# Dense layers that take a batch's tokens in the order in which the last Fourier stage makes them

## The chip, the cores and the metric

The kernel runs on one core of one Trainium2 chip. The metric is the device time of one execution in microseconds; lower is better. Engines are named as the profile names them: PE (TensorE; PEld are its weight loads), DVE (VectorE), ACT (ScalarE), POOL (GpSimd) and SP (SyncE, which here only issues DMAs).

## The reference, cut to what matters

```python
def _attn_ref(x, filt_r, filt_i):                # x: (8, 3008, 256)
    X = np.fft.rfft(x, axis=1)
    Y = X * (filt_r + 1j * filt_i)[None, :, :]
    return np.fft.irfft(Y, n=x.shape[1], axis=1)

def _moe_ref(x, w_in, w_out):                    # x: (24064, 256); 256 -> 2048 -> 256
    h = x @ w_in
    g = 0.5 * h * (1.0 + erf(h / np.sqrt(2.0)))
    return g @ w_out
```

Each of the 8 batches is filtered along its 3008 positions in the frequency domain, and then every position ("token") goes through two dense layers with an exact Gelu between them. The dense layers treat each token by itself, so they may take the tokens in any order, if each result is stored in its own row.

## The kernel before, in words

**Fourier part.** 3008 is 47 x 64. The transform and its inverse are made of small matrix products. Batch 0 has its own code (`c1` to `c4`), which runs before the main loop. Batches 1 to 7 are computed in four stages that lie between the dense layers' matmuls:

- `s1(b, c)`, four chunks: eight matmuls into four PSUM banks (three of pool `f`, one of pool `h`), drained to `a_sb` by DVE and ACT, and stored by SP to a DRAM buffer `R1`. `r1` loads it back in another layout (`b_sb`).
- `s2(b, p)`, twelve units: two matmuls into one `f` bank; DVE multiplies it with the filter `F` (line 428) into `p`.
- `s3(b, u)`, three units: sixteen matmuls into three `f` banks and one `h` bank; `s3_out` drains them to `v_sb` in two halves, the second half one slot later, and SP stores them to a DRAM buffer `R2`. `r2(b, c)` loads it back as `d_sb`, in four chunks.
- `s4(b, grp, half)`, sixteen units (8 groups of 4 columns, times 2 halves of the channels): four matmuls of 94 columns into one `f` bank, drained by DVE or ACT into the ring `y_sb`.

A token's place in its batch is 32 m + w, with m from 0 to 93 and w from 0 to 31. One `s4` group makes the four values of w from 4 grp to 4 grp + 3 for all 94 m. In the kernel before, the drain puts them at their natural places: runs of four elements, 32 apart. So a dense tile of 512 tokens in a row needs all eight groups.

**Dense part.** The tokens of all batches are cut into 47 tiles of 512 (`TCH`); 5.875 tiles make a batch, so most batches begin within a tile. `mm1(t, jc)` makes one sixteenth of tile t's hidden layer: two matmuls of 512 columns from the ring into an `h` bank and a Gelu on ACT into `g_sb` (line 589). The second layer is done by `mm2_seven` with seven block products in the place of eight: 112 matmuls of 128 columns a tile on PE (line 659) and sums of quarters on DVE (`sums_1` to `sums_3`, lines 628, 634, 641). The results are gathered by DVE in `t_sb` and `ost` (lines 674 to 688) and stored by SP, two stores of 256 rows for each tile (line 690).

**Order.** The order of every engine's work is written out by hand. The main loop has 16 slots for each tile. In slot 16 t + jc the kernel first issues what `put` has noted for that slot, then seven matmuls of `mm2_seven(t - 1)`, then `mm1(t, jc)`. Tile 5, the first to hold tokens of batch 1, is an exception: its `mm1` begins only at slot 86, and in the slots 80 to 85 the second layer of tile 4 goes twice as fast. `first(b)` is the first slot of the first tile that holds tokens of batch b. All of `s4(b)` ends before that slot:

```python
            s1, n1, r1, s2, n2, group, r2, s4, n4 = hi - 94, 3.7, hi - 80, hi - 71, 3.4, 14, hi - 25, hi - 17, 1
        unit = lambda p: s2 + group * (p // 4) + int(n2 * (p % 4))
        for u in range(16):
            put(s4 + int(u * n4), m.s4, b, u // 2, u % 2)
```

Each engine works in the order in which the instructions were issued to it. SP's one queue holds, in this order of issue, the `R1` and `R2` stores, the `r1` and `r2` loads and the stores of the result. PSUM has 3 banks for `h`, 2 for `ps_o`, 3 for `f`; the `f` banks are shared by `s1` to `s4`.

Of the kernel before, what the change touches and what calls it, by code (L numbers as in the profile page):

```python
# [20 lines left out]
HB = 32  # L21
RND = 12582912.0
TCH = 512
TURNS = 64.0


def _dram(src, off, dims):
    return dataclasses.replace(src, offset=src.offset + off, ap=[list(d) for d in dims])


class _Mix:
# [433 lines left out]
    def s4(self, b, grp, half):  # L465
        nc = self.nc
        o = b % 2 * self.S
        d = self.st[b, "d", grp // 2]
        ps = self.bank("ps_s4")
        for i in range(4):  # L470
            nc.tensor.matmul(ps[:, 94 * i:94 * i + 94],  # L471
                             lhsT=d[:, (grp % 2) * 4 + i, 128 * half:128 * half + 128],
                             rhs=self.T4a[:, 4 * grp + i], start=True, stop=True)
        yv = self.ring[:, half, o:o + self.S].rearrange("c (m w) -> c m w", w=HB)[:, :, 4 * grp:4 * grp + 4]
        pv = ps[:, 0:376].rearrange("c (i m) -> c m i", i=4)
        self._evac(yv, pv, "act" if half or b == 1 and grp > 3 else False, 1.0 / self.S)

# [75 lines left out]
    def c4(self, u, eng):  # L553

        if u == 0:

            self.ring = self.py.tile([128, 2, 2 * self.S], BF16, tag="y", name="y_sb")
        d = self.st[0, "d", u // 2]
        for half in range(2):
            ps = self.bank("ps_c4", "h" if (2 * u + half) % 5 < 3 else "o")  # L560
            for i in range(4):
                self.nc.tensor.matmul(ps[:, 94 * i:94 * i + 94],
                                      lhsT=d[:, 4 * (u % 2) + i, 128 * half:128 * half + 128],
                                      rhs=self.T4c.rearrange("p a b -> p (a b)"), start=True, stop=True)
            yv = self.ring[:, half, 0:self.S].rearrange("c (m w) -> c m w", w=HB)[:, :, 4 * u:4 * u + 4]
            self._evac(yv, ps[:, 0:376].rearrange("c (i m) -> c m i", i=4), eng[half], 1.0 / self.S)


# [22 lines left out]
    def mm2(self, t, s):  # L591
        nc = self.nc
        tile_i, q = s // 4, s % 4
        g = self.st["g", t]
        if s % 8 == 0:
            self.st["o"] = self.bank("ps_o", "o").rearrange("p (a b) -> p a b", a=2)
        ps = self.st["o"]
        for i in range(4):
            jc = 4 * q + i
            nc.tensor.matmul(ps[:, tile_i % 2, :], lhsT=g[:, jc, tile_i * 128:tile_i * 128 + 128],  # L600
                             rhs=self.w_out_sb[:, jc, :], start=(jc == 0), stop=(jc == 15))
        if s % 8 == 7:
            ost = self.po.tile([128, 2, 256], FP32, tag="ost", name="ost")
            nc.vector.tensor_copy(out=ost, in_=ps)
            r0 = t * TCH + (tile_i - 1) * 128
            nc.sync.dma_start(out=self.out[r0:r0 + 256, :].rearrange("(s p) o -> p s o", p=128), in_=ost)

    def weight_sums(self):

# [33 lines left out]
    def mm2_seven(self, t, lo, hi):  # L643

        nc, v = self.nc, self.nc.vector.tensor_tensor
        a11, a12, s2, a22 = self.quarters(t)
        w = self.w_out_sb.rearrange("p (i k) (n o) -> p k n i o", k=2, n=2)
        q = self.w_sums
        s31, s4 = self.st["s", t], self.st.get(("s4", t))
        ops = ((a11, w[:, 0, 0]), (a12, w[:, 1, 0]), (s2, q[:, 1]), (s31[:, :, 0], q[:, 2]),  # L650
               (s31[:, :, 1], q[:, 0]), (a22, q[:, 3]), (s4, w[:, 1, 1]))
        last = t == self.B * self.S // TCH - 1
        for n in range(lo, hi):
            m, sub, i = n // 16, n // 8 % 2, n % 8
            if n % 16 == 0 and (m == 0 or m % 2 == 1) or last and m > 4 and i == 0:
                self.st["o"] = self.bank("ps_o", "h" if n > 80 else "o").rearrange("p (m s o) -> p m s o", m=2, s=2)
            ps = self.st["o"]
            a, b = ops[m]
            nc.tensor.matmul(ps[:, (m + 1) % 2, sub, :], lhsT=a[:, i, 128 * sub:128 * sub + 128], rhs=b[:, i],  # L659
                             start=i == 0, stop=i == 7)  # L660
            if last and m > 4 and i == 7:
                self.finish(t, m, sub, ps)
            if n % 16 != 15 or m % 2 or last and m > 4:
                continue
            p0, p1 = ps[:, 0], ps[:, 1]
            if m == 0:
                self.st["t"] = self.po.tile([128, 2, 2, 128], FP32, tag="ost", name="t_sb")
                self.st["c"] = [None, None]
            if m in (2, 4):
                self.st["c"][m // 4] = self.po.tile([128, 2, 256], FP32, tag="ost", name="ost")  # L670
            t1, t3 = self.st["t"][:, 0], self.st["t"][:, 1]
            c = lambda h, k: self.st["c"][h][:, :, 128 * k:128 * k + 128]
            if m == 0:
                nc.vector.tensor_copy(out=t1, in_=p1)
            elif m == 2:
                v(out=c(0, 0), in0=t1, in1=p0, op=ALU.add)  # L676
                if last:
                    self.store(t, 0, 0, nc.sync)
                v(out=t1, in0=t1, in1=p1, op=ALU.add)
            elif m == 4:  # L680
                v(out=t3, in0=t1, in1=p0, op=ALU.subtract)  # L681
                v(out=c(1, 1), in0=t3, in1=p1, op=ALU.add)
                if last:
                    self.store(t, 1, 1, nc.scalar)
                v(out=t1, in0=t1, in1=p1, op=ALU.add)
            else:
                for h, tt, p in ((1, t3, p0), (0, t1, p1)):
                    v(out=c(h, 1 - h), in0=tt, in1=p, op=ALU.add)  # L688
                    r0 = t * TCH + 256 * h
                    nc.sync.dma_start(out=self.out[r0:r0 + 256, :].rearrange("(s p) o -> p s o", p=128),  # L690
                                      in_=self.st["c"][h])

    def store(self, t, h, k, eng):
        r0, k = t * TCH + 256 * h, slice(128 * k, 128 * k + 128)
        eng.dma_start(out=self.out[r0:r0 + 256, k].rearrange("(s p) o -> p s o", p=128), in_=self.st["c"][h][:, :, k])

    def finish(self, t, m, sub, ps):

        h = 6 - m
        c, tt = self.st["c"][h], self.st["t"][:, h]  # L700
        k = slice(128 * (1 - h), 128 * (1 - h) + 128)
        self.nc.vector.tensor_tensor(out=c[:, sub, k], in0=tt[:, sub], in1=ps[:, (m + 1) % 2, sub], op=ALU.add)
        if h == 1:
            if sub == 1:
                self.store(t, 1, 0, self.nc.sync)
            return
        r0 = t * TCH + 128 * sub
        (self.nc.sync if sub else self.nc.scalar).dma_start(out=self.out[r0:r0 + 128, k], in_=c[:, sub, k])


@with_exitstack
def kernel(
# [9 lines left out]
    m = _Mix(ctx, tc, x, filt_r, filt_i, moe_w_in, moe_w_out, out)  # L722
    nc, B, S = tc.nc, m.B, m.S
# [114 lines left out]
    def put(slot, f, *a):  # L838
        at.setdefault(slot, []).append((f, a))
# [4 lines left out]
    for b in range(1, B):  # L844
        hi = first(b)
        if b == 1:
            s1, n1, r1, s2, n2, group, r2, s4, n4 = 0, 3, 12, 27, 2.5, 12, 64, 73, 0.75
        elif b == 2:
            s1, n1, r1, s2, n2, group, r2, s4, n4 = hi - 92, 3.7, hi - 78, hi - 70, 3.4, 14, hi - 24, hi - 17, 1
        else:  # L850
            s1, n1, r1, s2, n2, group, r2, s4, n4 = hi - 94, 3.7, hi - 80, hi - 71, 3.4, 14, hi - 25, hi - 17, 1
        unit = lambda p: s2 + group * (p // 4) + int(n2 * (p % 4))
        for u in range(16):
            put(s4 + int(u * n4), m.s4, b, u // 2, u % 2)
        for c in range(4):
            put(s1 + int(c * n1), m.s1, b, c)
            put(r1 if c < 3 else unit(3) + 1, m.r1, b, c)
            put(r2 if c < 3 else s4 + int(4 * n4) + 1, m.r2, b, c)
        for p in range(12):
            put(unit(p), m.s2, b, p)  # L860
            if p % 4 == 3:
                put(unit(p) + 3, m.s3, b, p // 4)
                put(unit(p) + 4, m.s3_out, b, p // 4, 1)
        if b + 1 < B:
            for i in range(8):
                put(unit(i + 2) if b > 1 else 25, m.load_next, b, i + 2, i // 2, i % 2)
# [20 lines left out]
    for s in range((NT + 1) * 16):  # L887
        t, jc = s // 16, s % 16
# [41 lines left out]
```

## Time and profile before

| | |
|---|---|
| median of 3 runs | 751.09 us (751.04 to 751.09) |
| the profiled execution: its time | 751.4 us |
| the profiled execution: its span, first to last instruction | 749.5 us |
| mean granted clock of TensorE | 0.999 |
| busy share of PE, DVE, ACT, POOL | 97%, 79%, 73%, 14% |
| Gelu, `g_sb<-ps_h`, 752 of 512 columns | 599 ns each |
| drain of `s4`, `y_sb<-ps_s`, 376 columns | 545 ns on DVE, 481 ns on ACT |
| filter product `p<-ps_s,F` on DVE (84) | 1220 ns each |
| stores of the result on SP | 92 of 256 KB, 3.0 us to landing, and three smaller at the end |
| `d_sb<-R` on SP (56) | 192 KB, 3.9 us to landing |
| DMA issues on SP, all | 333 |

The span is some 2 us less than the execution's time, since launch and end lie around it. The profile's busy time of PE is made from modelled ends of matmuls, so the distance from one start to the next says more than a duration. A line number is that of the kernel before; helper lines stand for many callers (303, 305 and 307 are the drains of `_evac`), so tiles are named with them.

### The profile page before, as it was taken

The numbers are of one execution on the slowest core, as the hardware profiler recorded it, in microseconds if no ns is written. First come the engines' busy times: TensorE is split into PE (matmuls) and PEld (weight loads), VectorE is DVE, ScalarE is ACT, GpSimd is POOL, SyncE is SP. The second block draws the span as 40 slices with busy tenths as digits, with TensorE's granted clock in tenths as the row PEclk, the third lists the DMA queues.
The fourth block names the chain that finished last, engine by engine and source line by source line (L and its number), as shares of the span: only waits on it lengthen the run. The fifth ranks groups of instructions, "written<-read, shape, count | busy, mean of one in ns | idle before, by whom it ended". The sixth has DMA issues, their size and how long they took to land.

```text
span 749.5 us, 20005 instructions
## 1 busy us (share of the span) xinstructions
PE 729.1 (97%) x8286; PEld 517.9 (69%) x8420; DVE 588.9 (79%) x1053; ACT 548.6 (73%) x975; POOL 105.2 (14%) x195
## 2 busy tenths in 40 slices
PE   7999999999999999999999999999999999999998
PEld 4855666766776667666777666666677766777776
DVE  7978866897787977789777996779967798666566
ACT  6986678777786778766787667876678767777773
POOL 7979100020001200012000120002100000000000
PEclk9999999999999999999999999999999999999999
DMA  9998653565354652546625557245562432501011
GB/s 150 219 221 241 151 142 93 165 127 118 92 129 142 142 130 80 157 118 120 148 71 157 112 106 170 61 146 121 125 142 72 135 107 76 124 29 58 30 57 58
DMA packets 90187, 90.70 MB, mean 121 GB/s; under 512 B 6768, under 2 KB 76912, under 8 KB 89840
## 3 DMA queue, kind: packets, MB, share of 16 engines
q1 hardware_dynamic: 82000, 72.18, 34.9%
q0 software_dynamic: 7680, 17.04, 14.5%
q8 instruction: 66, 1.08, 0.6%
q10 hardware_dynamic: 416, 0.20, 0.1%
q14 instruction: 25, 0.20, 0.1%
HBM read 57.15 MB, written 48.23 MB: 141 GB/s over the span
## 4 chain that ended last, share of the span: by engine, by line
PE 84%; DVE 6%; DMA 4%; ACT 2%; issue 2%; POOL 0%; SPq 0%; DVEq 0%; POOLq 0%; ACTq 0%
PE ps_o L659 36%; PE ps_h L586 35%; PE ps_s L471 3%; PE ps_s L442 3%; PE ps_s L425 2%; PE ps_s L398 2%; DVE p L428 2%; DVE s_sb L628 2%; DMA R<-v_sb 2%; ACT g_sb L589 2%; DMA d_sb<-R 2%; DMA x_sb<-in_x_dram 1%; PE ps_c L533 1%; PE ps_c3t L548 1%; PE ps_c L511 0%
## 5 line engine op out<-in xcount | busy, mean ns | idle before, releaser
L589 ACT ACTIVATE g_sb<-ps_h 128x512 f16<-128x512 f32 x752 | 446.6, 599 | 181.9 <-PE ps_h L586 158.7
L586 PE MATMUL ps_h<-y_sb,w_in_sb 128*128 128x512 bf16 (+3 forms) x1470 | 417.5, 365 | 0.4
L659 PEld LDWEIGHTS <-g_sb 128*128 128x128 f16 x2944 | 193.9, 98 | 78.8 <-issue 14.8
L659 PEld LDWEIGHTS <-s_sb 128*128 128x128 f16 x2208 | 150.0, 98 | 51.6 <-issue 3.5
L586 PEld LDWEIGHTS <-w_in_sb 128*128 128x128 bf16 x1600 | 124.8, 98 | 8.0 <-issue 1.0
L659 PE MATMUL ps_o<-w_sums,g_sb 128*128 128x128 f16 x1472 | 127.3, 219 | 1.2 <-DVE g_sb L634 0.4
L659 PE MATMUL ps_o<-w_sums,s_sb 128*128 128x128 f16 x1472 | 125.8, 219 | 1.2
L628 DVE TENSOR_TENSOR s_sb<-g_sb 128x1024 f16<-128x1024 f16 x184 | 123.5, 695 | 0.3 <-ACT g_sb L589 0.3
L659 PE MATMUL ps_o<-w_out_sb,g_sb 128*128 128x128 f16 x1472 | 119.8, 219 | 2.1 <-DVE ost L688 0.4
L428 DVE TENSOR_TENSOR p<-ps_s,F 128x1024 bf16<-128x1024 f32 x84 | 102.5, 1220 | 20.3 <-PE ps_s L425 19.0
L122 POOL COPY gate<-p 1x1 bf16<-1x1 bf16 x40 | 18.7, 468 | 416.5 <-DVE p L428 416.5
L634 DVE TENSOR_TENSOR g_sb<-s_sb,g_sb 128x1024 f16<-128x1024 f16 x92 | 63.6, 691 | 1.1
L659 PE MATMUL ps_o<-w_out_sb,s_sb 128*128 128x128 f16 x736 | 63.8, 219 | 0.5
L641 DVE TENSOR_TENSOR s_sb<-g_sb 128x1024 f16<-128x1024 f16 x92 | 63.0, 684 | 0.0
L307 DVE TENSOR_SCALAR y_sb<-ps_s 128x376 bf16<-128x376 f32 x52 | 28.3, 545 | 27.7 <-PE ps_s L471 27.7
L471 PEld LDWEIGHTS <-d_sb 96*128 96x128 bf16 x448 | 31.2, 98 | 26.4 <-issue 2.6
L681 DVE TENSOR_TENSOR t_sb<-t_sb,ps_o 128x256 f32<-128x256 f32 x46 | 19.2, 416 | 38.3 <-PE ps_o L659 38.3
L305 DVE CAST a_sb<-ps_s 128x512 bf16<-128x512 f32 x57 | 36.6, 686 | 14.8 <-PE ps_s L398 14.6
L676 DVE TENSOR_TENSOR ost<-t_sb,ps_o 128x256 f32<-128x256 f32 x46 | 19.3, 419 | 33.6 <-PE ps_o L659 33.4
L471 PE MATMUL ps_s<-T4a,d_sb 96*128 96x94 bf16 x448 | 37.4, 206 | 2.7 <-DMA d_sb<-R 1.4
L688 DVE TENSOR_TENSOR ost<-t_sb,ps_o 128x256 f32<-128x256 f32 x90 | 33.6, 414 | 6.4 <-PE ps_o L659 6.4
L86 POOL DMA_DIRECT2D x_sb<-in_x_dram x64 | 32.9, 520 | 3.1 <-issue 2.9
(148 smaller groups left out, 508.7 us busy)
## 6 DMA issues: line engine op xcount, KB each, us to landing
out_dram<-ost SPq DMA_DIRECT2D x92, 256.0 KB, 3.0
x_sb<-in_x_dram POOLq DMA_DIRECT2D x64, 188.0 KB, 3.8
b_sb<-R SPq DMA_DIRECT2D x28, 384.0 KB, 4.0
R<-v_sb SPq DMA_DIRECT2D x84, 128.0 KB, 2.5
d_sb<-R SPq DMA_DIRECT2D x56, 192.0 KB, 3.9
R<-a_sb SPq DMA_DIRECT2D x54, 192.0 KB, 3.0
F<-Fd SPq DMA_DIRECT2D x4, 512.0 KB, 9.7
Fd<-F SPq DMA_DIRECT2D x8, 192.0 KB, 6.9
```

The costliest lines, as they stand in the source:

```text
L86: nc.gpsimd.dma_start(out=xt[h * o:h * o + NA, w:w + 8, :], in_=xv[h][:, w:w + 8, :])
L305: self.nc.vector.tensor_copy(out=out, in_=in_)
L307: self.nc.vector.tensor_scalar(out=out, in0=in_, scalar1=scale, scalar2=None, op0=ALU.mult)
L428: nc.vector.tensor_tensor(out=w, in0=ps.unsqueeze(1).to_broadcast([128, 2, 512]), in1=self.F[:, :, 2 * p:2 * p + 2, :].rearrange("p t a b ...
L471: nc.tensor.matmul(ps[:, 94 * i:94 * i + 94], lhsT=d[:, (grp % 2) * 4 + i, 128 * half:128 * half + 128], rhs=self.T4a[:, 4 * grp + i], sta ...
L586: nc.tensor.matmul(ps[:, o:o + n], lhsT=w[:, dc], rhs=self.ring[:, dc, off:off + n], start=(dc == 0), stop=(dc == 1))
L589: nc.scalar.activation(out=self.st["g", t][:, jc, :], in_=ps, func=AF.Gelu)
L628: self.nc.vector.tensor_tensor(out=self.st["s", t][:, i:i + 2], in0=a, in1=b, op=ALU.subtract)
L634: self.nc.vector.tensor_tensor(out=a21[:, k], in0=self.st["s", t][:, k, 0], in1=a22[:, k], op=ALU.add)
L641: self.nc.vector.tensor_tensor(out=self.st["s4", t][:, k], in0=a12[:, k], in1=s2[:, k], op=ALU.subtract)
L659: nc.tensor.matmul(ps[:, (m + 1) % 2, sub, :], lhsT=a[:, i, 128 * sub:128 * sub + 128], rhs=b[:, i], start=i == 0, stop=i == 7)
L688: v(out=c(h, 1 - h), in0=tt, in1=p, op=ALU.add)
```

## The change

- Within the ring a batch's tokens now stand group by group: group `grp` is the 376 places from `GRP * grp` (94 m times 4 w). The `s4` and `c4` drains write 376 elements in a row.
- A dense tile of 512 places needs the one, two or three groups that it touches. `s4` is spread over the tiles: `due(u)` is the first slot of the first tile that uses group u, and its two halves are put 3 slots apart, the first of them 5 to 14 slots ahead of it (1 for batch 1's first). `r2` of chunk c comes 9 slots (8 for the last chunk) before the first group that uses it. So `s4` of a batch now lies in the same slots as `s1`, `s2` and `s3` of the next one.
- `s1`, `s2`, `s3` and their loads start 6 slots later for batches 2 to 7; for batch 1 the `s2` units stand 3 slots apart in groups of 14 slots, in the place of 2.5 and 12.
- The results of a tile belong to rows of the output in groups of four. `put_rows` stores 128 places at a time, cut where a group ends: runs of four rows of 1 KB, 32 rows apart. There are 253 stores of results in the place of 95; 249 are issued by SP and 4, at the end, by ACT (2 before).

The diff, without the three other places where `put_rows` takes the place of a store (`mm2`, `store`, `finish`):

```diff
+GRP = 376
...
@@ s4
-        yv = self.ring[:, half, o:o + self.S].rearrange("c (m w) -> c m w", w=HB)[:, :, 4 * grp:4 * grp + 4]
+        o += GRP * grp
+        yv = self.ring[:, half, o:o + GRP].rearrange("c (m w) -> c m w", w=4)
@@ c4
-            yv = self.ring[:, half, 0:self.S].rearrange("c (m w) -> c m w", w=HB)[:, :, 4 * u:4 * u + 4]
+            yv = self.ring[:, half, GRP * u:GRP * u + GRP].rearrange("c (m w) -> c m w", w=4)
@@ mm2_seven
-                    r0 = t * TCH + 256 * h
-                    nc.sync.dma_start(out=self.out[r0:r0 + 256, :].rearrange("(s p) o -> p s o", p=128),
-                                      in_=self.st["c"][h])
+                    for sub in range(2):
+                        self.put_rows(t * TCH + 256 * h + 128 * sub, self.st["c"][h][:, sub], nc.sync)
+
+    def put_rows(self, r0, tile_, *engines, k=slice(0, 256)):
+
+        lo, hi = r0, r0 + 128
+        for eng in engines * 4:
+            if lo == hi:
+                return
+            b, i = divmod(lo, self.S)
+            n = min(hi - lo, GRP - i % GRP)
+            o = b * self.S + 4 * (i // GRP) + HB * (i % GRP // 4)
+            w = k.stop - k.start
+            out = _dram(self.out, o * self.D + k.start, [[HB * self.D, n // 4], [self.D, 4], [1, w]])
+            eng.dma_start(out=out, in_=tile_[lo - r0:lo - r0 + n])
+            lo += n
+        assert lo == hi
@@ the kernel's schedule
         if b == 1:
-            s1, n1, r1, s2, n2, group, r2, s4, n4 = 0, 3, 12, 27, 2.5, 12, 64, 73, 0.75
+            s1, n1, r1, s2, n2, group = 0, 3, 12, 27, 3, 14
         elif b == 2:
-            s1, n1, r1, s2, n2, group, r2, s4, n4 = hi - 92, 3.7, hi - 78, hi - 70, 3.4, 14, hi - 24, hi - 17, 1
+            s1, n1, r1, s2, n2, group = hi - 86, 3.7, hi - 72, hi - 64, 3.4, 14
         else:
-            s1, n1, r1, s2, n2, group, r2, s4, n4 = hi - 94, 3.7, hi - 80, hi - 71, 3.4, 14, hi - 25, hi - 17, 1
+            s1, n1, r1, s2, n2, group = hi - 88, 3.7, hi - 74, hi - 65, 3.4, 14
         unit = lambda p: s2 + group * (p // 4) + int(n2 * (p % 4))
-        for u in range(16):
-            put(s4 + int(u * n4), m.s4, b, u // 2, u % 2)
+
+        due = lambda u: (b * S + GRP * u) // TCH * 16
+        pair = lambda u: 0 <= u < 7 and due(u + 1) == due(u)
+        s4 = lambda u: due(u) - ((1 if b == 1 else 10 if pair(0) else 5) if u == 0 else 14 if pair(u) else
+                                 5 if pair(u - 1) else 8)
+        for u in range(8):
+            for half in range(2):
+                put(s4(u) + 3 * half, m.s4, b, u, half)
         for c in range(4):
             put(s1 + int(c * n1), m.s1, b, c)
             put(r1 if c < 3 else unit(3) + 1, m.r1, b, c)
-            put(r2 if c < 3 else s4 + int(4 * n4) + 1, m.r2, b, c)
+            put(s4(2 * c) - (9 if c < 3 else 8), m.r2, b, c)
```

More of the change, by code (lines that the diff above doesn't have):

```diff
@@ L604, in mm2 @@
             nc.vector.tensor_copy(out=ost, in_=ps)
-            r0 = t * TCH + (tile_i - 1) * 128
-            nc.sync.dma_start(out=self.out[r0:r0 + 256, :].rearrange("(s p) o -> p s o", p=128), in_=ost)
+            for sub in range(2):
+                self.put_rows(t * TCH + (tile_i - 1 + sub) * 128, ost[:, sub], nc.sync)
     def weight_sums(self):
@@ L688, in mm2_seven @@
                     v(out=c(h, 1 - h), in0=tt, in1=p, op=ALU.add)
-                    r0 = t * TCH + 256 * h
-                    nc.sync.dma_start(out=self.out[r0:r0 + 256, :].rearrange("(s p) o -> p s o", p=128),
-                                      in_=self.st["c"][h])
+                    for sub in range(2):
+                        self.put_rows(t * TCH + 256 * h + 128 * sub, self.st["c"][h][:, sub], nc.sync)
[12 more added lines that the diff above has]
+        assert lo == hi
     def store(self, t, h, k, eng):
-        r0, k = t * TCH + 256 * h, slice(128 * k, 128 * k + 128)
-        eng.dma_start(out=self.out[r0:r0 + 256, k].rearrange("(s p) o -> p s o", p=128), in_=self.st["c"][h][:, :, k])
+        k = slice(128 * k, 128 * k + 128)
+        for sub in range(2):
+            self.put_rows(t * TCH + 256 * h + 128 * sub, self.st["c"][h][:, sub, k], eng, k=k)
     def finish(self, t, m, sub, ps):
@@ L706, in finish @@
             return
-        r0 = t * TCH + 128 * sub
-        (self.nc.sync if sub else self.nc.scalar).dma_start(out=self.out[r0:r0 + 128, k], in_=c[:, sub, k])
+        engines = (self.nc.sync, self.nc.scalar)
+        self.put_rows(t * TCH + 128 * sub, c[:, sub, k], *(engines if sub else engines[::-1]), k=k)
 @with_exitstack
```

## The prediction

> **What bounds the kernel now.** First the page: its totals and the chain that ended last.
>
> ```profile
> span 749.5 us, 20005 instructions
> PE 729.1 (97%) x8286; PEld 517.9 (69%) x8420; DVE 588.9 (79%) x1053; ACT 548.6 (73%) x975; POOL 105.2 (14%) x195
> ...
> PE 84%; DVE 6%; DMA 4%; ACT 2%; issue 2%; POOL 0%; SPq 0%; DVEq 0%; POOLq 0%; ACTq 0%
> ```
>
> TensorE is the bound: 97% busy, 84% of the chain. Second the stretches, to see where TensorE does more than its pure work: two batches from first Gelu to first Gelu, one tile without Fourier work, and two tiles of a batch's middle (columns: stretch, its length, busy us of PE, PEld, DVE, ACT, POOL, clock, DMA share, GB/s).
>
> ```profile
> 206.94:297.64 90.70, 89.79 (x1050) 64.68 (x1064) 73.93 (x131) 66.99 (x119) 7.56 (x16) 1.00 0.50 123
> ...
> 388.25:479.72 91.47, 89.78 (x1050) 65.54 (x1064) 73.93 (x131) 66.97 (x119) 7.56 (x16) 1.00 0.51 122
> 674.91:688.07 13.16, 13.05 (x146) 9.38 (x146) 8.00 (x18) 9.55 (x16) 0.00 (x0) 1.00 0.12 41
> ...
> 236.69:252.06 15.37, 15.14 (x167) 10.44 (x168) 14.67 (x26) 10.60 (x18) 4.36 (x10) 1.00 0.68 148
> 267.41:282.02 14.61, 14.45 (x170) 10.04 (x171) 10.49 (x23) 10.91 (x20) 0.00 (x0) 1.00 0.64 154
> ```
>
> Six pure tiles are 6 x 13.16 = 79.0 us, so a batch's transform adds 11.7 us to 90.7. Of that `s4` is 64 matmuls that start 47 ns apart, 3.0 us: full rate, no wait. A batch from 2 on has nothing to gain by spreading `s4`. VectorE is 95% busy in the stretch 236.69 to 252.06 (`s2`, `s3`) and 72% in the next but one, where `s4` starts. Third the timeline: where TensorE really waits.
>
> ```profile
> 69.85 0.62 PE L442 MATMUL ps_s<-p,U 64*64 64x512 bf16 x7 [0.83 <-DVE p L428]
> ...
> 71.02 0.51 PE L659 MATMUL ps_o<-w_sums,g_sb 128*128 128x128 f16 x6 [0.38 <-DVE g_sb L634]
> ...
> 83.66 0.62 PE L442 MATMUL ps_s<-p,U 64*64 64x512 bf16 x7 [1.02 <-ACT v_sb L303]
> ...
> 106.51 0.51 PE L471 MATMUL ps_s<-T4a,d_sb 96*128 96x94 bf16 x8 [0.41 <-DMA d_sb<-R]
> ...
> 118.32 1.05 PE L398 MATMUL ps_s<-x_sb,T1s 47*64 47x512 bf16 x8
> 118.43 0.49 ACT L303 ACTIVATE y_sb<-ps_s 128x376 bf16<-128x376 f32 x1 [0.48 <-PE ps_s L471]
> ...
> 207.66 0.63 PE L398 MATMUL ps_s<-x_sb,T1s 47*64 47x512 bf16 x8
> ...
> 461.86 0.34 PE L471 MATMUL ps_s<-T4a,d_sb 96*128 96x94 bf16 x4 [0.83 <-DMA d_sb<-R]
> ```
>
> By start-to-start gaps against the normal step, these are 1.1, 0.6, 1.3, 0.4 (batch 1) and 0.8 us (batch 5). The rows at 118.32, 118.43 and 207.66 are the price that I use most: eight `s1` matmuls take 0.63 us, but 1.05 us where an `s4` unit stands just before them, since they wait until ScalarE has emptied its bank: **0.42 us**. Everything to be won is some 6 us.
>
> **What the Trainium skill says.** "PSUM — Partial Sum Buffer", Specifications: eight banks, a matmul's output fits one. The kernel uses 3 + 2 + 3; the 1.05 us row agrees that three `f` banks are few. "Perfetto Trace Analysis", Tensor Engine Instruction: the end of a matmul is estimated, and ScalarE and VectorE are strict FIFO; hence I count starts, and a drain waits for what is queued before it (at 207.77 a Gelu begins 0.1 us after `s1`, and its drains only after it). "DMA: Bandwidth & Descriptors", Latency and other measured facts: the receipt round trip to the memory dominates a DMA's fixed cost. It agrees: 128 KB of `v_sb` land after 2.5 us, 256 KB of output after 3.0. So more, smaller stores cost issue time, not latency.
>
> **The change, part by part.** Slots are the steps of the main loop (0.82 us pure); what is put at a slot runs before that slot's own matmuls.
>
> *At nothing:* the contiguous ring write. ScalarE takes 481 ns for 376 elements and 599 for 512, 0.87 ns an element; VectorE 545 and 686, 1.04: no sign of a charge for the 8-byte runs. No gain, no loss; 0.05 us each way would hide behind TensorE. Bytes and 1 KB rows of the stores stay. Matmul counts stay.
>
> *Gains, batch 1.* `s2` starts come at 27, 30, 33, 36 instead of 27, 29, 32, 34, groups of 14 slots instead of 12. VectorE, continuously busy from 59.2 to 71 (the row at 69.85 ends that), gets 1.65 us but has to do one `g_sb` (1.24) and a copy (0.41) before the last product: the wait for `p` stays 1.1, the 0.6 for `g_sb` goes. The 1.3 at 83.66 is an `s3` whose third `f` bank is its own first one; in the changed program's bank assignment it gets three different ones: -1.3. The `s1` row at 118.32: -0.4. Waits for `d_sb`: `r2` of chunk 0 alone instead of three together, and in batches 3 to 5 18 slots from the last `s3_out` to `s4` instead of 12: -0.2, -0.8, -0.1. A wait of 0.35 for L688 in the last batch: gone. Sum **-3.7** (0 to -6).
>
> *Losses: `s4` among `s1`, `s2`, `s3` of the next batch, on three `f` banks.*
> (a) An `s4` in the slot of an `s1`, whose third `f` bank is the one `s4` just filled: slots 184, 187, 280, 283, 379, 475, 568, 571. Five are VectorE drains, 0.42 + 0.06 = 0.48; three are ScalarE drains behind a running Gelu, 0.6: **+4.2** (2 to 6).
> (b) Slots 427 and 523: `s4`, then `s2` on the very same bank. VectorE starts 0.24 after the last matmul (118.19 to 118.43) and drains for 0.55: +0.8 each, **+1.6** (1 to 3).
> (c) Slots 126, 235, 331, 619: `s2` after `s4` after `s3` takes the bank that VectorE drains second (0.69 each), where before it had one drained by ScalarE: 0.4 at 126, where an L628 lies between, 0.15 elsewhere: **+0.85** (0 to 3).
> (d) Slots 139, 440, 536, 632: `s4` before `s3`, needed nine matmuls (0.6 us) later: **+0.9** (0 to 2).
> (e) VectorE: `y_sb` drains (0.55 each, one or two a tile) now fall into the 95% busy tiles; slots gain only 0.2 of TensorE each: **+0.7** (0 to 5).
> (f) Slots 80 to 82, where `mm2` runs at double rate: three `s4` units (0.19 each) no longer stand ahead of the `g_sb` that VectorE ended at 116.69, TensorE used at 116.75: **+0.55** (0 to 1).
>
> *Stores.* 95 become 253 (249 on SP, 4 on ScalarE's queue at the end); SP issues 487 DMAs instead of 333. Back to back they take 0.48 us each (449.28, 449.77), so five or six stores hold SP for 2.5 to 3 us, not 1. Behind them queue `R` writes and `r2`. `r2` at the slot after the stores (144, 608, 704; chunk 3): stores begin 0.56 us after the Gelu of that slot, five of them and two loads end 3.6 us in, landing 3.9 later (the median): 7.5 us, when `s4` is due eight slots (6.7 us and what else is in them) later: 0.35, 0.15, 0.75: **+1.2** (0 to 3). Two slots later they have 2 us to spare. The wait of a store for VectorE holds only SP. The tail stays: the last two stores go on two queues.
>
> Sum: 4.2 + 1.6 + 0.85 + 0.9 + 0.7 + 0.55 + 1.2 = 10.0; less 3.7, **+6.3 us**. The profiled execution is 751.4 us (span 749.5), the median 751.09; 751.1 + 6.3 = **757.4 us**.
>
> **The rivals.** *Faster:* the drains come back in time, so that (a) to (d) cost a third, 2.5 us, (e) and stores nothing, and batch 1 loses even its 1.1: 751.1 - 4.8 + 3.0 = 749.3, at best 746. For it: before, no wait from batch 2 on is long. It decides where a drain ends within the 0.4 us of five `s1` matmuls; the row at 118.32 speaks against. *VectorE becomes the bound:* each of six batches loses 1 us more in the `s2` tiles, since 14.67 + 0.55 of 15.37 us leaves nothing: 763. *SP becomes the bound:* ten `r2` are issued within two slots after five or six stores; at 0.6 us an issue and the longest landing of `d_sb` (5.6 us) each would be 1 to 2 us late: 770. Against it: q1 holds the 16 engines for 34.9% of the span only, and seven of the ten have 2 us of slack. *Nothing to measure:* losses at their lower ends equal the gains, 751.
>
> **How the numbers follow.** A measurement tells about 0.2%, 1.5 us, from no change. Likeliest case (752.6 to 761) 0.49, VectorE 0.14, SP 0.10: slower 0.73. Within 1.5 us 0.10. Faster 0.17. The likeliest case's own range is 753 to 761; the range for 8 in 10 leaves out half of the faster case and most of SP's: 748.5 to 764.
>
> **What would show it.** Right: in the waits, `ps_s` L399 waiting for `y_sb` drains, `ps_s` L426 too; batches 2 to 5 near 92 us instead of 90.7; the tile with `s4`'s old place shorter (15.6 to about 14), the `s2` tiles longer; the 83.66 row gone; L705 with 249 issues on SP. Wrong: batch periods of 90.7 or less mean that the drains are hidden; waits for `d_sb` over 1 us mean SP; p L429 and ost L690 among what TensorE waits for mean VectorE.

## The result, and the profile after

The changed kernel takes **767.59 us** (median; 767.15 to 768.39) beside 751.07 us (750.62 to 751.09) of the kernel before: ratio 1.0223 [1.0205, 1.0240], 16.5 us slower. The forecast was slower by 6.3 us, at most 764: right in sign, wrong in size.

The page of the kernel after: its totals and the chain that ended last.

```profile
span 765.8 us, 20240 instructions
PE 736.9 (96%) x8286; PEld 520.2 (68%) x8420; DVE 586.3 (77%) x1053; ACT 550.1 (72%) x975; POOL 103.2 (13%) x195
...
PE 74%; DVE 10%; DMA 7%; issue 3%; ACT 2%; POOL 2%; SPq 1%; DVEq 0%; POOLq 0%; ACTq 0%
```

TensorE does the same matmuls (8286 recorded in both profiles) in a span 16.3 us longer; its share of the chain falls from 84% to 74%, VectorE's rises from 6% to 10% and that of DMAs from 4% to 7%. Some 3 points of TensorE's fall and 2 of the DMAs' rise lie ahead of the main loop, where the chain only takes another path: the first Gelu stands at 39.31 us, before at 39.41. The rest is waiting. The list of waits of the kernel after names it (columns: total us, times, longest; PEld and PE on the same line are mostly the same wait seen twice):

```profile
PEld L661 <- DVE g_sb L636: 6.8, 13, 1.7
PEld L472 <- DMA d_sb<-R: 6.6, 4, 1.9
...
PE ps_s L472 <- DMA d_sb<-R: 4.9, 5, 1.4
...
PE ps_s L426 <- DVE y_sb L308: 1.3, 2, 0.6
...
PE ps_s L399 <- ACT y_sb L304: 1.0, 3, 0.3
```

The rows of the kernel before that belong to the first two:

```profile
PE ps_s L471 <- DMA d_sb<-R: 1.4, 3, 0.8
...
PEld L659 <- DVE g_sb L634: 0.8, 2, 0.5
```

The waits of `s1` (L399) and `s2` (L426) for `y_sb` drains are the bank waits that the prediction was about. The list shows only a part of them, since it counts idle time behind the modelled ends of matmuls; from start to start they are 5.6 us. The waits of `s4` (L472) for `d_sb` were to be over 1 us only if SP was the trouble: it was. Next the stretches (columns as in the prediction's table): of the kernel after two batches, a tile with two `s4` units and nothing else, and the last tile; then the last tile of the kernel before:

```profile
207.07:299.82 92.75, 91.05 (x1050) 64.85 (x1064) 73.50 (x131) 67.43 (x119) 6.89 (x16) 1.00 0.50 120
392.53:485.08 92.55, 90.61 (x1050) 65.97 (x1064) 73.70 (x131) 67.25 (x118) 7.16 (x16) 1.00 0.50 120
686.28:699.80 13.52, 13.36 (x153) 9.75 (x154) 8.55 (x19) 9.93 (x17) 0.00 (x0) 1.00 0.25 69
742.45:765.83 23.38, 18.23 (x238) 14.56 (x238) 13.47 (x30) 9.45 (x16) 0.00 (x0) 0.98 0.23 69
```

```profile
727.55:749.50 21.95, 18.52 (x243) 14.79 (x243) 13.76 (x31) 9.56 (x16) 0.00 (x0) 0.98 0.23 74
```

The first of the two batches takes 92.75 us instead of 90.70, the second 92.55 instead of 91.47 (forecast: near 92). The tile with two `s4` units takes 13.52, one without any took 13.16: 0.18 each, their bare work. Up to tile 11 nothing is lost (its first Gelu stands at 207.07, before at 206.94): what batch 1 gains pays for what is lost up to there. The end loses 1.43 us that no term of the sum had. Two kinds of stall in the timeline of the kernel after; first an `s4` just ahead of an `s1` (left: start, duration):

```profile
216.47 0.34 PE L472 MATMUL ps_s<-T4a,d_sb 96*128 96x94 bf16 x4
...
216.74 0.62 PE L399 MATMUL ps_s<-x_sb,T1s 47*64 47x512 bf16 x5
217.17 0.48 ACT L304 ACTIVATE y_sb<-ps_s 128x376 bf16<-128x376 f32 x1
...
217.69 0.41 PE L399 MATMUL ps_s<-x_sb,T1s 47*64 47x512 bf16 x3 [0.34 <-ACT y_sb L304]
```

`s1` stops after five matmuls until the drain that stood behind a Gelu is done; start to start the sixth comes 0.65 us late. Then `r2` behind the stores:

```profile
712.37 0.76 DVE L690 TENSOR_TENSOR ost<-t_sb,ps_o 128x256 f32<-128x256 f32 x2 [0.39 <-PE ps_o L661]
...
712.82 3.92 SPq L705 DMA_DIRECT2D out_dram<-ost  x5
...
716.84 1.10 SPq L463 DMA_DIRECT2D d_sb<-R  x2
...
720.62 0.35 PE L472 MATMUL ps_s<-T4a,d_sb 96*128 96x94 bf16 x4 [1.27 <-DMA d_sb<-R]
```

Five stores hold SP for 3.92 us, the two loads follow, and TensorE goes on 3.8 us after the first of them was issued; in the kernel before such a load landed after 3.9 (median), so it isn't the load that is slow here. The prediction had the same five stores at 0.48 us each, 2.4 in all.

### The profile page after: what moved, and what is told of

The parts are those of the page before. It is cut to its first block, busy times and chain, and to the rows that moved or that the text cites. A ratio compares the mean times of both kernels' runs of the same rounds, so it can differ in the third digit from the quotient of the medians.

```text
span 765.8 us, 20240 instructions
## 1 busy us (share of the span) xinstructions
PE 736.9 (96%) x8286; PEld 520.2 (68%) x8420; DVE 586.3 (77%) x1053; ACT 550.1 (72%) x975; POOL 103.2 (13%) x195
## 3 DMA queue, kind: packets, MB, share of 16 engines
q8 instruction: 66, 1.08, 0.6%
## 4 chain that ended last, share of the span: by engine, by line
PE 74%; DVE 10%; DMA 7%; issue 3%; ACT 2%; POOL 2%; SPq 1%; DVEq 0%; POOLq 0%; ACTq 0%
PE ps_o L661 33%; PE ps_h L588 32%; DVE s_sb L630 3%; DMA d_sb<-R 3%; PE ps_s L472 3%; PE ps_s L443 3%; DVE p L429 2%; PE ps_s L399 2%; DVE g_sb L636 2%; ACT g_sb L591 2%; DMA x_sb<-in_x_dram 2%; PE ps_s L426 1%; POOL x_sb L87 1%; DMA F<-in_filt_i_dram 1%; DMA R<-v_sb 1%
## 5 line engine op out<-in xcount | busy, mean ns | idle before, releaser
L661 PEld LDWEIGHTS <-g_sb 128*128 128x128 f16 x2944 | 196.9, 98 | 84.8 <-DVE g_sb L636 6.8
L661 PEld LDWEIGHTS <-s_sb 128*128 128x128 f16 x2208 | 147.4, 98 | 53.2 <-issue 10.3
L661 PE MATMUL ps_o<-w_sums,g_sb 128*128 128x128 f16 x1472 | 128.9, 219 | 5.5 <-DVE g_sb L636 3.0
L123 POOL COPY gate<-p 1x1 bf16<-1x1 bf16 x40 | 16.7, 418 | 432.7 <-DVE p L429 432.7
L472 PEld LDWEIGHTS <-d_sb 96*128 96x128 bf16 x448 | 31.3, 98 | 30.7 <-DMA d_sb<-R 6.6
L472 PE MATMUL ps_s<-T4a,d_sb 96*128 96x94 bf16 x448 | 37.9, 206 | 5.9 <-DMA d_sb<-R 4.9
L690 DVE TENSOR_TENSOR ost<-t_sb,ps_o 128x256 f32<-128x256 f32 x90 | 33.7, 417 | 8.0 <-PE ps_o L661 8.0
L426 PE MATMUL ps_s<-b_sb,T2p 128*128 128x256 bf16 x168 | 32.0, 272 | 1.9 <-DVE y_sb L308 1.3
```

The lines of the kernel that those rows point to most:

```text
L426: nc.tensor.matmul(ps[:, 256 * i:256 * i + 256], lhsT=self.T2p[:, k].rearrange("p a b c d -> p (a b c d)"), rhs=self.st[b, "b", k // 6][:, ...
L472: nc.tensor.matmul(ps[:, 94 * i:94 * i + 94], lhsT=d[:, (grp % 2) * 4 + i, 128 * half:128 * half + 128], rhs=self.T4a[:, 4 * grp + i], sta ...
```

## The experiments

All times are medians with the ratio to the kernel before, which took 750.7 to 751.07 us beside them.

**r2_early**: the loads away from the stores, nothing else.

```diff
-            put(s4(2 * c) - (9 if c < 3 else 8), m.r2, b, c)
+            put(s4(2 * c) - (13 if c else 9), m.r2, b, c)
```

> Kernel after, but the loads r2 of chunks 1 to 3 of every batch are issued 13 slots ahead of their s4 instead of 9 or 8, so that none stands on SP behind the five or six stores of a tile half or behind a wait for R1. Theory SP (the loads of d_sb are late because the stores occupy SP's queue just ahead of them): the four long d_sb waits (184.14, 611.18, 633.68, 720.62 us; 1.34 + 1.09 + 0.85 + 1.22 us beyond the normal step) go, so 767.6 - 4.5 = 763 us (762 to 764.5). Rival, traffic (the loads land late because the transfers themselves are slow, whatever SP's order): the waits stay, 766.5 to 768.

Measured: 762.87 us, 1.0157 [1.0141, 1.0172]; 4.7 us less than the kernel after. The four long waits are gone. By the starts of the Gelus around them they were 1.55, 1.30, 1.08 and 1.45 us, 5.4 in all and some 0.2 more each than the expectation has; two other waits came out 0.4 longer each, one of them in batch 1, whose first load was not moved (109.70 us). Loads issued four or five slots sooner would have hidden slow transfers too, so this run alone doesn't tell SP's order from them; the next one, where the loads keep their slots and their bytes, does for the waits that it takes away.

**stores_before**: the stores of the kernel before, the schedule of the kernel after.

```diff
-            for sub in range(2):
-                self.put_rows(t * TCH + 256 * h + 128 * sub, self.st["c"][h][:, sub], nc.sync)
+            r0 = t * TCH + 256 * h
+            nc.sync.dma_start(out=self.out[r0:r0 + 256, :].rearrange("(s p) o -> p s o", p=128), in_=self.st["c"][h])
...
```

> Kernel after with the stores of the kernel before: one DMA of 256 consecutive rows for each half tile (the results so land in rows in another order than the reference's). SP issues 158 fewer DMAs. Theory SP: the d_sb waits that stand behind stores shrink (some 3 of 4.5 us; the one at 611 us stands behind a wait for R1 and stays), and the end, where the last store lands 4.5 us after VectorE's last sum instead of 2.8, comes 1.4 to 1.7 us nearer: 762.5 to 763.5 us. Rival, the stores cost nothing of their own (order of s4 is all): 767 to 768.

Measured: 762.11 us, 1.0147 [1.0132, 1.0163]. The last tile is back at 21.94 us, and of the waits for `d_sb` those at the slots 152 and 594 are left in part (0.95 and 1.03 us); those at 616 and 712 are gone. At 152 the first load is issued at 178.06 and TensorE goes on only 5.9 us later, so there the loads themselves have a part. So in this schedule the new stores cost 5.5 us, and the schedule with the old stores costs 11.0. The wait at 594 is mostly not the stores' doing: there `r2` stands behind three loads `b_sb` of 384 KB, and TensorE gets its data only 6.3 us after the first `d_sb` load is issued (604.87 to 611.18 in the kernel after).

**dodge**: `s4` out of the slots of `s1`, `s2`, `s3`.

```diff
-                put(s4(u) + 3 * half, m.s4, b, u, half)
+                late_s4.append((s4(u) + 3 * half, b, u, half))
...
+    busy = {s for s in at for f, a in at[s] if f in (m.s1, m.s2, m.s3)}
+    for s, *a in late_s4:
+        put(s + (s in busy), m.s4, *a)
```

> Kernel after, but an s4 unit whose slot holds an s1, s2 or s3 too is put one slot later (same work, same engines). Theory banks (terms a to d of the prediction: TensorE waits for the f bank that s4 has just filled): s1 waits 4.2, s2 waits 1.6 + 0.6 and s3 waits some 1 us go for the most part: 767.6 - 6 = 761.5 us (760.5 to 764). Rival, VectorE is the limit in these tiles: what the banks give back is lost in waits for g_sb: 766 to 768.

Measured: 761.12 us, 1.0144 [1.0127, 1.0162]; 6.5 us less, on four runs from 759.80 to 763.11. The timeline of dodge at the place shown above: `s1` runs clear, and the `s4` has the time after it.

```profile
212.51 0.63 PE L399 MATMUL ps_s<-x_sb,T1s 47*64 47x512 bf16 x8
...
213.91 0.34 PE L472 MATMUL ps_s<-T4a,d_sb 96*128 96x94 bf16 x4
```

The gain isn't lost to VectorE.

**order_only**: the new token order and the new stores, every other stage where the kernel before has it.

```diff
-            s1, n1, r1, s2, n2, group = hi - 88, 3.7, hi - 74, hi - 65, 3.4, 14
+            s1, n1, r1, s2, n2, group, r2, s4, n4 = hi - 94, 3.7, hi - 80, hi - 71, 3.4, 14, hi - 25, hi - 17, 1
...
+        for u in range(16):
+            put(s4 + int(u * n4), m.s4, b, u // 2, u % 2)
```

> The schedule of the kernel before (s1, s2, r2, s4 in their old slots, s4 in one run) with the new token order and the new stores of groups of four rows. Theory (s4 spread is most of the loss, the stores cost only where r2 stands behind them and at the end): 751.1 + 1.4 (end) + 0 to 1.5 = 752.5 to 754 us. Rival, the stores alone are the loss (SP's queue late everywhere): 758 or more. Rival, the stores cost nothing: 751.

Measured: 770.02 us, 1.0258 [1.0242, 1.0273]. My number missed by 16 us, and the rival that I had put at 758 or more holds. The waits that order_only adds are of one sort:

```profile
PE ps_s L472 <- DMA d_sb<-R: 10.9, 6, 3.6
...
PEld L472 <- DMA d_sb<-R: 5.1, 3, 1.9
...
PE ps_s L426 <- DMA b_sb<-R: 4.8, 4, 1.9
```

Both loads that come over SP, `r1` and `r2`, are late in nearly every batch; tile 11, where `s1` stands clear of `s4`, takes 15.83 us (before: 15.88). With stores and schedule both old or new there are four kernels:

| | old stores | new stores |
|---|---|---|
| old schedule | 751.1 | 770.0 |
| new schedule | 762.1 | 767.6 |

The new stores cost 19.0 us on the old schedule and 5.5 on the new one. The new schedule (`s4` and `r2` spread, `s1` to `s3` moved) costs 11.0 by itself and hides 13.5 of what the stores cost.

**before_253**: why a store is dear. The kernel before, its stores cut into the same pieces but with consecutive rows.

```diff
+            n = min(hi - lo, GRP - lo % self.S % GRP)
+            eng.dma_start(out=self.out[lo:lo + n, k], in_=tile_[lo - r0:lo - r0 + n])
```

> Kernel before, its stores cut into the same 253 pieces as the kernel after has, but of consecutive rows (output as the reference's). In the kernel after an issue of a store takes SP 0.71 us on the mean (249 make 176.9 us), in the kernel before 0.45 (90 make 40.9 us). Theory form (the four-row pattern makes an issue longer): here a store takes about 0.45 again, 112 us of SP, and the time lies well below order_only's 770: 753 to 760 us. Rival, number (an issue close behind another is slow, whatever its rows): about 0.7 us a store and the same late loads as in order_only: 768 to 771.

Measured: 755.55 us, 1.0058 [1.0043, 1.0073]. The means below are of SP's 249 store records in each trace:

| SP, one store | pieces of 128 rows (128) | shorter pieces (121) | all |
|---|---|---|---|
| consecutive rows (before_253) | 0.46 us | 0.45 us | 0.455 us, sum 113.4 us |
| groups of four rows (after) | 0.62 us | 0.80 us | 0.711 us, sum 176.9 us |

Five stores in a row, in the timeline of before_253, to be read beside the five of 3.92 us above:

```profile
452.20 2.10 SPq L700 DMA_DIRECT2D out_dram<-ost  x5
```

The number of issues costs 4.8 us on the old schedule, their form the other 14.5 up to order_only.

**after_flat**: the same edit of the row pattern in the kernel after.

```diff
-            out = _dram(self.out, o * self.D + k.start, [[HB * self.D, n // 4], [self.D, 4], [1, w]])
-            eng.dma_start(out=out, in_=tile_[lo - r0:lo - r0 + n])
+            eng.dma_start(out=self.out[lo:lo + n, k], in_=tile_[lo - r0:lo - r0 + n])
```

> Kernel after, each of its 253 store pieces written to consecutive rows instead of groups of four (the results so land in another order than the reference's). Theory form (the number of issues was priced rightly and the price of one wrongly): a store takes SP 0.45 us as in before_253, so the waits for d_sb at the slots 152, 616 and 712 shrink to about what the prediction summed (1.2 us), and the end comes nearer: 763 us (762 to 764.5). Rival (the number alone makes r2 late): 766 to 768.

Measured: 763.16 us, 1.0162 [1.0148, 1.0176]; 4.4 of the stores' 5.5 us are the form. With a store at about the price that the prediction used, the waits at the slots 152, 616 and 712 are 0.68, 0 and 1.30 us beyond the normal step (the median step between the same two kinds of matmul), together 2.0 (predicted: 1.2); at 594 there is 0.83 left. The one at 712 isn't a matter of price: one of the five stores ahead of it took 2.05 us, and the trace doesn't show why.

**combo**: dodge and r2_early together (both edits above).

> Kernel after with both edits, s4 off the slots of s1, s2 and s3 (dodge, -6.5 us) and r2 of chunks 1 to 3 earlier (r2_early, -4.7 us). Theory (two separate causes): they add up, 767.6 - 11.2 = 756.4 us (755.5 to 758). Rival (one hides behind the other, or VectorE takes over): 759 to 761.

Measured: 755.83 us, 1.0069 [1.0057, 1.0081]; 11.8 us less than the kernel after, beside 4.7 + 6.5 = 11.2. The causes are separate. The longest row of what is left among TensorE's waits, here of combo and then of the next experiment:

```profile
PEld L661 <- DVE g_sb L636: 7.2, 14, 1.7
```

```profile
PEld L661 <- DVE g_sb L636: 4.7, 10, 1.4
```

**combo_act**: combo, and VectorE drains no `y_sb` in the main loop.

```diff
-            self._evac(yv, pv, "act" if half or b == 1 and grp > 3 else False, 1.0 / self.S)
+            self._evac(yv, pv, "act", 1.0 / self.S)
```

> combo, with all y_sb drains on ScalarE instead of half on VectorE. Theory (term e: the eight waits of 0.3 to 0.4 us and one of 0.5 for g_sb from batch 2 on come from y_sb drains in VectorE's queue): these go, -2.5 us, 753.3 us (752.5 to 754.5). Rival (ScalarE's drains then hold the Gelus and TensorE waits for ps_h or for the bank instead): 756 or more.

Measured: 753.01 us, 1.0028 [1.0018, 1.0037]; 2.8 us less than combo. From batch 2 on four waits for `g_sb` are gone (1.4 us); one of 0.3 us is left in each of the batches 3 to 6, one of 0.5 in batch 2 and one of 0.1 in batch 7, and TensorE waits for no `ps_h`. The rest of the gain is other waits, those of batch 1 and of two `s1` among them. One that is left, in the timeline of combo_act:

```profile
236.45 1.22 DVE L429 TENSOR_TENSOR p<-ps_s,F 128x1024 bf16<-128x1024 f32 x1
...
237.58 0.68 DVE L636 TENSOR_TENSOR g_sb<-s_sb,g_sb 128x1024 f16<-128x1024 f16 x1
...
238.31 0.34 PEld L661 LDWEIGHTS <-g_sb 128*128 128x128 f16 x6 [0.36 <-DVE g_sb L636]
```

Here the sum stands behind a filter product of `s2`, not behind a drain. This is the best version with the new order, and still slower than the kernel before.

**combo_tail** and **combo_end**: the end. In combo_tail POOL issues the stores of tile 45, in combo_end also the first two of tile 46.

```diff
-                                      nc.sync)
+                                      nc.gpsimd if t == self.B * self.S // TCH - 2 else nc.sync)
...
-                    self.store(t, 0, 0, nc.sync)
+                    self.store(t, 0, 0, nc.gpsimd)
...
-                    self.store(t, 1, 1, nc.scalar)
+                    self.store(t, 1, 1, nc.gpsimd)
```

> combo, and the stores of the last tile but one are issued by POOL, so that SP has only the last tile's behind it at the end. Theory (the end is late because eleven stores hold SP for 8.2 us): 1.2 us less than combo, 755.2 us (754.5 to 757). Rival (the last store's own way to memory sets the end): as combo within 0.3 us.

> combo_tail, and in the last tile the first two stores (the ones of h = 0, k = 0 and h = 1, k = 1) are issued by POOL too, so that SP and ScalarE's queue hold little ahead of the very last ones. Theory (the end is late by the issues of the last tile itself, six on SP and four on ScalarE's queue, 0.7 to 0.9 us each): 0.8 us less than combo_tail, 754.2 us. Rival (the last stores' own landing): 755 as combo_tail.

Measured: combo_tail 755.02 us, 1.0057 [1.0045, 1.0069]; combo_end 760.50 us, 1.0124 [1.0108, 1.0139]. In combo_tail the last tile takes 23.69 us, in combo 23.83: the difference of 0.8 us, for which the two intervals overlap, is not at the end (of the 2.0 us between the two profiles 1.0 lies ahead of the main loop, whose first Gelu starts at 39.25 instead of 40.29), so this run doesn't show what it was made for. The last queue to finish issuing was not SP's but ACT's, in combo (753.14 beside 752.16) and in combo_tail (751.19 beside 750.20); combo_tail took five stores off SP and none off ACT's queue, whose last store alone takes 1.43 us. In combo_end it is another thing: POOL's closing drain instruction (not counted as busy) begins while POOL issues its last stores (744.05 in combo_tail, 749.95 in combo_end) and ends 8.40 and 8.46 us later, at 752.45 and 758.41, and then the program ends. In combo_tail that is as late as SP's own end (752.37); in combo_end it is 4.3 us later (754.11). My expectation failed on that. What remains of the theory is what stores_before and after_flat show, that the end comes back with other stores.

**before_n3** and **before_r2**: can the gains be had without the change?

```diff
-            s1, n1, r1, s2, n2, group, r2, s4, n4 = 0, 3, 12, 27, 2.5, 12, 64, 73, 0.75
+            s1, n1, r1, s2, n2, group, r2, s4, n4 = 0, 3, 12, 27, 3, 12, 65, 74, 0.75
```

> Kernel before with one edit in batch 1: s2 three slots apart instead of 2.5 (groups of 12 as they were; r2 and s4 one slot later). Theory (most of the gain of the kernel after in batch 1 is the s3 at 83.66 us, which here too gets three different f banks): -1.3 us for that, -0.2 for the wait for p, up to +0.6 for d_sb: 749.8 us (749.2 to 750.6). Rival (the gain is tied to the groups of 14): 751.

Measured: 753.47 us, 1.0036 [1.0023, 1.0049]; slower. The wait of 1.3 us at 83.66 is gone, but with groups of 12 the next `s2` comes while the `s3` still has its banks, twice (timeline of before_n3), and 2.3 us of waiting for `d_sb` come out of 0.6, since the last `R2` store, one slot later, falls behind the two stores of a tile, and SP waits 1.65 us for it before it can issue the loads:

```profile
71.89 1.09 ACT L303 ACTIVATE v_sb<-ps_s 128x512 bf16<-128x512 f32 x2
...
73.03 0.38 PE L425 MATMUL ps_s<-b_sb,T2p 128*128 128x256 bf16 x2 [0.75 <-ACT v_sb L303]
```

So the edit by itself only moves the wait. (The profile is of the fastest of five runs, 751.91 us; it doesn't show what the median has beyond that.) In the kernel after the groups of 14 leave room for it, and its `s4` may come late; that both are needed is read from these two kernels, not tested apart.

```diff
-            ... hi - 94, 3.7, hi - 80, hi - 71, 3.4, 14, hi - 25, hi - 17, 1
+            ... hi - 94, 3.7, hi - 80, hi - 71, 3.4, 14, hi - 28, hi - 17, 1
```

> Kernel before, r2 of chunks 0 to 2 issued three slots earlier in batches 2 to 7. Theory (the waits for d_sb in batch 5 and later, 0.8 and 0.3 us, are r2's place on SP): they go, 749.9 us (749.5 to 750.6), which would beat both kernels. Rival (d_sb then waits for the last v_sb that R still misses): 751.

Measured: 751.08 us, 1.0001 [0.9992, 1.0009]: nothing. The wait in batch 5 shrinks from 0.77 to 0.28 us over the normal step, but one in batch 1, which the edit doesn't touch, came out 0.3 us longer and one for `b_sb` 0.1: waits of this size vary from run to run. No version beat the kernel before.

## Why the prediction was wrong in size

By its own steps; "measured" is the excess of a step between matmul starts over the normal step in the profile of the kernel after, unless another is named. The profiles of both kernels have no record of 134 of the 8420 matmuls, all of them of `mm1`; next to such a gap the starts of the Gelus were taken.

| step | predicted | measured |
|---|---|---|
| gains: batch 1, `d_sb`, L688 | -3.7 | -3.5 |
| (a) `s4` in the slot of `s1` | +4.2 | +4.0 |
| (b) `s2` on the bank of `s4` | +1.6 | +1.6 |
| (c) `s2` after `s4` after `s3` | +0.85 | +0.6, all at slot 126 |
| (d) `s4` before `s3` | +0.9 | +1.0 |
| (e) drains in VectorE's queue | +0.7 | +2.7 |
| (f) slots 80 to 82 | +0.55 | +0.8 |
| stores: `r2` late | +1.2 | +5.4 |
| stores: the end | 0 | +1.4 |
| not in the sum | | +0.9 |
| what is left of 16.3, in small steps, not assigned | | +1.4 |

**Right:** the mechanism of (a) to (d), bank by bank. The eight places of (a) came out as 0.41 (five VectorE drains) and 0.65 (three behind a Gelu), forecast 0.48 and 0.6; the two of (b) as 0.79. dodge takes most of them away and is 6.5 us faster; (a) to (d) measure 7.2. It also put new waits in (one of 1.1 us at slot 140). Right too: the 83.66 row is gone, and the contiguous drain changes nothing (545 and 549 ns on VectorE, 481 and 479 on ScalarE, before and after). Of the gains the one for `p` and `g_sb` in batch 1 was the most mis-sized: 1.7 us of waiting became 1.56, not 1.1.

**Wrong, the main step:** "Back to back they take 0.48 us each". That is the time of a whole store of the kernel before, whose rows are consecutive; the new pattern was taken as free because "Bytes and 1 KB rows of the stores stay". An issue of it takes 0.62 us for 128 rows and 0.80 for a piece cut at a group's edge. The row behind the 0.48, two whole stores of the kernel before:

```profile
449.28 0.90 SPq L690 DMA_DIRECT2D out_dram<-ost  x2
```

So the places were right (144, 608 and 704 of `r2`, seen as 1.55, 1.08 and 1.45 us at the slots 152, 616 and 712) and the sizes 1.2, 0.9 and 0.7 too small; and a fourth was missed. At slot 585 `r2` stands behind an `r1` that waits 2.26 us for the last `R1` store: 1.30 us at slot 594, of which 1.03 stay with the old stores, so that this one is mostly a matter of the order of the loads. r2_early takes all four away (5.4 us, 4.7 net), after_flat brings those of the prediction to 2.0.

"The tail stays" failed for the same reason. That the last two stores go on two queues was true; but SP has eleven of them to issue, 8.2 us from 754.48 on, and ACT's queue four, the last of which alone takes 1.44 us (0.64 at most in after_flat) and ends 1.0 us after SP's last, at 763.68. That is 2.4 us after VectorE's last sum instead of 0.4. The last issues of the kernel after, then of the kernel before:

```profile
759.38 3.30 SPq L705 DMA_DIRECT2D out_dram<-ost  x4
...
760.13 3.56 ACTq L705 DMA_DIRECT2D out_dram<-ost  x4
```

```profile
746.44 0.35 ACTq L708 DMA_DIRECT2D out_dram<-ost  x1
...
746.71 0.41 SPq L708 DMA_DIRECT2D out_dram<-ost  x1
```

after_flat and stores_before give the end back (22.14 and 21.94 us for the last tile).

**Wrong, second:** (e) was set at 0.7 us for all batches together, with the stretch 95% busy in view. From batch 2 on TensorE waits ten times for a `g_sb` sum, 0.2 to 0.5 us each (3.2 us), and once for a copy L690 (0.44); four waits of 0.24 for the same copy in the kernel before are gone: 2.7 net. Drains in VectorE's queue, the mechanism of (e), explain only a part of it: combo_act has none there and still keeps six such waits, 1.9 us. In five of them VectorE runs a filter product of `s2` right ahead of the sum, in the sixth one more sum lies between; and in the kernel after only two of the ten sums (0.36 us each) come right behind a `y_sb` drain, five right behind a filter product. The change moved `s2` by six slots too, and (e) had no price for that; a run with `s2` alone put back was not made, so this part is read from the order on VectorE, not shown. That combo_act's gain of 2.8 us is close to 2.7 is chance. Missed as well: two `s1` three slots after an `s4` (0.28 each) and a copy L690 in batch 1 (0.35), together the 0.9.

**The rivals.** SP as the bound (770) was half true: the delays of 1 to 2 us came, in four of ten places. In order_only, where `s4` of a batch stands in one run as before, they came in nearly every batch, and with them 770.0. The forecast 0.10 for it was too low, since its price was the one number that no row showed for the new pattern. VectorE as the bound (763) holds for 2.7 us, not for six.

Two slips of reading changed little. The kernel before has 97 stores of results, not 95 (95 are SP's alone). The wait at 106.51 us was 0.57 us from start to start, not 0.4; with it the `d_sb` gains were 1.3 us where 1.1 was forecast.

## What to carry to other kernels

Price a moved or split DMA by the queue that issues it, per issue and for its own address pattern; bytes that stay the same say nothing of that. Before spreading a stage over others, list which bank each unit takes from the shared pool, and move a unit by one slot where the bank's drain would stand in the way: that alone was worth 6.5 us here. A change of schedule and a change of stores that it needs have to be judged together: their costs were 11.0 and 19.0 us apart and 16.5 together.

## What was not expected of the hardware

- A DMA whose DRAM side is groups of four 1 KB rows took SP 0.62 us to issue for 128 rows, one with consecutive rows 0.46; with fewer rows, cut at a group's edge, 0.80 beside 0.45.
- POOL's closing drain behind its last stores ran 8.4 us (8.40 and 8.46), longer than those stores took to land (1.8 to 3.9 us). In combo_end that made the program end 4.3 us after SP was done.
- A few issues on SP take 2 us with no reason in the trace (2.05 us at 709.95 in after_flat). This stays open, and so do the 1.4 us of small steps.
